# Re-sorting the head of a fused attention and expert kernel: values before keys, and one step of the first tile between the two halves of the second

## The chip, the cores and the metric

The kernel runs on one core of a Trainium2 chip. The metric is the device time of one execution in microseconds (us); lower is better. TensorE is called PE below (PEld is its weight load), VectorE is DVE, ScalarE is ACT, GpSimd is POOL and SyncE is SP.

## What is computed

The reference is banded attention over 8 batches, 8 heads, 576 positions and a head dimension of 64, followed by one feed-forward layer with the ELU function on all 4608 tokens:

```
scores = q @ k^T / 8, kept where |i - j| <= 32, else -1e9
attn   = softmax(scores);  a = attn @ v
x = a.transpose(0, 2, 1, 3).reshape(4608, 512)
h = x @ w_in                      # 512 x 2048
g = where(h > 0, h, exp(min(h, 0)) - 1)
out = g @ w_out                   # 2048 x 512
```

All inputs and the output are float32; the kernel multiplies in bfloat16.

## The kernel before

**Units of work.** Attention goes by *pairs*: pair i is two blocks of 64 queries, all heads, so 128 tokens. There are 36 pairs. The feed-forward layer goes by *tiles* of 256 tokens, two pairs to a tile, 18 tiles. Each tile has 8 *steps*; a step is 256 of the 2048 hidden columns. The list `order` (line 700) gives the order of the steps kk = 0, 1, 2, ...: steps 0 and 1 are the first two of tile 0, steps 2 and 3 the first two of tile 1, steps 4 and 5 the third and fourth of tile 0, steps 6 and 7 those of tile 1, and so on. From tile 2 on the tiles follow one another.

**One pair.** `scores` (line 372) makes the products of queries and keys in PSUM; `exponential` (393) applies the exponential on ACT. For the first four pairs `band` (360) has written a large negative number outside the band ahead of the products; later pairs are multiplied by a mask (`mask`, 400). `pv` (409) multiplies by the values, with a column of ones that gives the denominators; `normalize` (423) divides on DVE (a reciprocal, line 426, and a product, line 429). `x_transpose` (434) turns the 128 tokens' x on PE into PSUM, and `x_evac` (451) copies it to the bfloat16 tile xT, on ACT or DVE as its argument says (`copy_on`, lines 289 to 293).

**One step.** `mm1` (706) makes h in PSUM: 8 matmuls of 256 tokens (line 744), or, for steps 2 and 3, twice 8 matmuls of 128 tokens, one set for each pair of tile 1 (`BY_PAIRS`). `exponents` (750) takes the exponential on ACT (line 754) and calls `subtract` (759), which takes 1 off: on ACT for steps 1, 3 and 4 (line 764), on DVE for the rest (line 766; for step 0 only later, inside `elu`). `elu` (769) joins both branches on DVE and writes the tile g (line 777). `mm2(n)` (823) adds step n's g times w_out to the tile's two sums psY, 128 tokens each, in 4 matmuls of 512 columns (line 797).

**Order.** The schedule is written out by hand (`manual_schedule`): each engine runs its instructions in the order in which the program emits them. `at(kk, slot, fn, ...)` (572) puts a function into a slot of step kk: "half" is after the first 4 of the 8 matmuls of `mm1`, "mid" after `mm1` with its exponents, "dve" before it, "end" at the end. The loop at line 850 emits, for each step: `elu` of a listed step, slot "dve", `mm1`, slot "mid", `mm2` of listed steps, slot "end". Two small dictionaries (lines 852 and 864) change the lists in the first steps.

**The head.** Lines 484 to 545 are emitted ahead of the loop. Queries and keys of batch 0 come in three parts: HALF_A first through SP's and ACT's queues, FRONT_B through POOL's queue as a load that converts (`load_cast`, line 138, tile c), FRONT_C later. `transpose_qk` (328) turns a part on PE and copies it to qT or kT; `front_transpose` (472) does so in two halves, each with an engine and a PSUM tag of its own. Pairs 0 and 1 need HALF_A alone; pairs 2 and 3 need FRONT_B. Values come as V_e and V_o, two layouts that differ by 64 rows; in the first batch POOL loads V_o (`load_v_odd`, 157) and DVE copies parts of it to V_e (`rotate_back`, 163).

**POOL's queue.** Lines 488 to 501 and 547 to 559 issue the loads that convert: parts of q and k, values, and the weights. `load_w_in(c, z, nz)` (197) loads part z of nz of the c-th quarter (512 columns) of w_in; `load_w_out` likewise. After the last part of w_in a small load on SP's queue (`gate`, line 192) holds back SP's loads of the next batches' q and k (tile f).

**PSUM.** Tiles are named by tag: "s" and "u" have two banks, "y0", "y1", "h0", "h1" one. The tag "u" is given up at step 5 (`swap_pools`, line 84), and its two banks become "h2" and "t0", the sums of tile 1; tile 0's sums are "y0" and "y1". A tile of a tag waits until the readers of the tag's former tile are done.

Of the kernel before, what the change touches and what calls it, by code (L numbers as in the profile page):

```python
# [21 lines left out]
def kernel(  # L22
# [9 lines left out]
    nc = tc.nc  # L32
# [86 lines left out]
    FRONT_B = ((NC * HJ, HJ - 2), (NC * HJ, HJ - 1))  # L119
# [37 lines left out]
    def load_v_odd(b, m):  # L157
        lo = 128 * m + WIN
        nc.gpsimd.dma_start(  # L159
            out=V_o[b % 3][:, m, :, 0:D],  # L160
            in_=v[b, :, lo:lo + 128, :].rearrange("h p d -> p h d"))

    def rotate_back(b, m0, m1, parts=(0, 1)):
        e, o = V_e[b % 3], V_o[b % 3]
        for z in parts:
            nc.vector.tensor_copy(e[64 * (1 - z):64 * (2 - z),
                                    m0 + z:m1 + z],
                                  o[64 * z:64 * (z + 1), m0:m1])
# [28 lines left out]
    def load_w_in(c, z=0, nz=1):  # L197
        w = D_FF // 4 // nz
        c = c * nz + z
        nc.gpsimd.dma_start(  # L200
            out=w_in_sb[:, :, c * w:(c + 1) * w],
            in_=moe_w_in[:, c * w:(c + 1) * w].rearrange(
                "(o p) f -> p o f", p=128))
# [124 lines left out]
    def transpose_qk(b, which, part, j0, n, evac, tag="t0", later=None,  # L328
                     pt=None):
        z, nj = part  # L330
        if pt is None:
            pt = ps_tile([128, 1024 if n <= 8 else 2048], BF16, tag, "ptx")
        for j in range(n):
            if (b, which, z) in qk_c:
                for h in range(2):
                    nc.tensor.transpose(
                        pt[64 * h:64 * (h + 1), j * 128:(j + 1) * 128],
                        qk_c[b, which, z][:, h, (j0 + j) * D:
                                          (j0 + j + 1) * D], ident)
            else:  # L340
                nc.tensor.transpose(  # L341
                    pt[:, j * 128:(j + 1) * 128],
                    qk_b[b, which, z][:, j0 + j, :], ident)

        def evict(d=None, rows=NC, pitch=S):
            d = keys_or_queries(b, which) if d is None else d
            copy_on(evac,
                    _bap(d, [d.ap[0], [pitch, HP], [nj, rows], [1, n]],
                         z + j0),
                    _bap(pt, [pt.ap[0], [1, HP], [HP, rows], [128, n]]))  # L350

        if later is None:
            evict()
        else:
            later.append(evict)
# [4 lines left out]
    def band(i, tag):  # L360
        psS = ps_tile([128, 2, 512], FP32, tag, "psS")
        banded[i] = psS, tag
        step = QB if i == 0 else 0
        for par in range(2):
            nc.tensor.matmul(
                _bap(psS, [psS.ap[0], [128, HP], [QB, 2], [1, QB]], par * 512),
                lhsT=ident,
                rhs=_bap(far, [far.ap[0], [0, HP], [step, 2], [1, QB]],
                         QB - step),
                start=True, stop=False)  # L370
# [38 lines left out]
    def pv(i):  # L409
        psS, pu, pm, _, _ = st[i]  # L410
        for h in range(H):
            hp, par = h // 2, h % 2
            for z in range(2):
                jb = 2 * i + z
                b, qb = jb // NQB, jb % NQB
                vv = (V_e if qb % 2 == 0 else V_o)[b % 3]
                nc.tensor.matmul(  # L417
                    psS[QB * z:QB * (z + 1), par, hp * VD:(hp + 1) * VD],
                    lhsT=pm[:, par * HP + hp, z * QB:(z + 1) * QB],
                    rhs=vv[:, qb // 2, h, :],  # L420
                    start=True, stop=True)
# [12 lines left out]
    def x_transpose(i, bank=None):  # L434
        x_st, tag = st[i][3:]
        tag = bank or tag
        pt = ps_tile([128, NDO, 128], BF16, tag, "psXT")
        for do in range(NDO):
            nc.tensor.transpose(
                pt[:, do, :], x_st[:, 2 * do:2 * do + 2, :], ident)  # L440
        st[i] = pt
# [9 lines left out]
    def x_evac(i, eng=nc.vector):  # L451
        copy_on(eng, xT_of(i), st.pop(i))
# [19 lines left out]
    def front_transpose(which, part, evacs, tags, later=None):  # L472
        for (j0, n), evac, tag in zip(split(part), evacs, tags):
            transpose_qk(0, which, part, j0, n, evac, tag, later)
# [13 lines left out]
    for which in range(2):  # L488
        load_cast(0, which, FRONT_B[which])
    load_w_in(0, 0, 2)  # L490
    for m in (2, 3):
        load_v_odd(0, m)
    for z in (2, 3):
        load_w_in(0, z, 4)
    load_w_in(1)
    load_w_out(0, 0, 2)
    load_w_out(0, 1, 2)
    load_v(0, 4, HIGH)
# [6 lines left out]
    BOTH = (nc.scalar, nc.vector)  # L505
# [16 lines left out]
    for m in range(2):  # L522
        for z in range(2):
            rotate_back(0, m, m + 1, (z,))
    pv(0)
    front_transpose(0, FRONT_B[0], (nc.scalar, nc.scalar), ("h0", "h1"),
                    later := [])
    pv(1)
    later.pop(0)()
    for i in (0, 1):  # L530
        normalize(i)
    later.pop(0)()
    front_transpose(1, FRONT_B[1], BOTH, ("y0", "y1"))
    for i in (0, 1):
        x_transpose(i, f"h{i}")
        x_evac(i, BOTH[i])
        if i == 0:
            band(2, "s")
    scores(2)
    exponential(2)  # L540
    band(3, "u")
    scores(3)
    exponential(3)
    rotate_back(0, 2, 3)
    rotate_back(0, 3, 4, (0,))

    load_w_in(2, 0, 2)
    load_w_out(1, 1, 2)
# [23 lines left out]
    def at(kk, slot, fn, *args):  # L572
        tasks.setdefault((kk, slot), []).append((fn, args))

    def run(kk, slot):
        for fn, args in tasks.get((kk, slot), ()):
            fn(*args)
# [7 lines left out]
        at(kk + 2, "end", x_evac, i, nc.scalar)  # L585


    for i in (2, 3):
        at(0, ("half", "mid")[i - 2], pv, i)
        at(0, ("half", "mid")[i - 2], normalize, i)  # L590
    at(1, "half", x_transpose, 2, "y0")
    at(1, "half", x_evac, 2, nc.scalar)
    at(1, "mid", x_transpose, 3, "y1")
    at(1, "mid", x_evac, 3, nc.vector)
    at(5, "dve", swap_pools)


# [36 lines left out]
    for i in range(4, NPAIR):  # L634
        two = i >= FIRST_TWO
        kk, z = begin[i], i % 2 if two else 0
# [68 lines left out]

    def mm1(kk):
        t, s = order[kk]
        if kk == BY_PAIRS[1]:
            return
        ks = BY_PAIRS if kk == BY_PAIRS[0] else (kk,)  # L710
        tags = ((f"h{kk % 2}", "s") if kk == NSTEP - 1 else
                ("s",) if kk == 2 else ("u",) if kk == 3 else (f"h{kk % 2}",))
        for k in ks:
            psH[k] = []
        for z, tag in enumerate(tags):
            for k in ks:
                psH[k].append(ps_tile([128, FG // len(tags), TT], FP32,
                                      tag if k == kk else "u", "ps"))
        for p in range(len(ks)):
            for k in ks:  # L720
                for z in range(len(tags)):
                    products(k, z, p if len(ks) > 1 else None)
                if p == len(ks) - 1:
                    for z in range(len(tags)):
                        exponents(k, z)
                        if k == NSTEP - 1:
                            elu(k, z)


    BY_PAIRS = (2, 3)  # L730

    def products(kk, z, pair):
        t, s = order[kk]
        ps = psH[kk][z]
        w = ps.shape[1]
        for j in range(w):
            fo = s * FG + z * w + j
            for do in range(NDO):
                if pair is None:
                    o, r = ps[:, j, :], xT[t][:, :, do, :]  # L740
                else:
                    o = ps[:, j, pair * 128:(pair + 1) * 128]
                    r = xT[t][:, pair, do, :]
                nc.tensor.matmul(  # L744
                    o, lhsT=w_in_sb[:, do, fo * 128:(fo + 1) * 128],
                    rhs=r, start=(do == 0), stop=(do == NDO - 1))
            if j == 0 and pair is None:
                run(kk, "half")
# [100 lines left out]

    for kk in range(NSTEP):  # L850
        run(kk, "first")
        for n in {1: (), 2: (0, 1), 9: ()}.get(kk, (kk - 1,)):
            if n >= 0:
                elu(n)
        run(kk, "dve")
        mm1(kk)
        run(kk, "mid")
        if kk == NSTEP - 1:
            last_sums()
        elif kk >= LATE + LAG:  # L860
            for _ in range(3 if kk < LATE + LAG + 4 else 4):
                add(*todo.pop(0))
        else:
            for n in {2: (), 3: (), 4: (), 5: (0, 2), 6: (1, 3), 7: (4,),
                      8: (5, 6)}.get(kk, (kk - LAG,) if kk >= LAG else ()):
                run(kk, n)
                mm2(n)
        run(kk, "end")
# [30 lines left out]
```

## Time and profile before

| | us |
|---|---|
| median of 3 runs | 302.36 (302.04 to 302.88) |
| the profiled execution | 303.15 |
| its span, first to last instruction | 301.4 |
| PE busy in the span | 291.4 |
| DVE, ACT, POOL busy | 241.2, 169.0, 56.8 |
| start of step 0's matmuls (L744) | 15.38 |
| start of steps 2 and 3's matmuls | 19.00 |
| start of the first sums (L797) | 22.54 |

The granted TensorE clock was 0.998 of full speed in the mean. In a row of the timeline the columns are: start, duration, engine, line, operation, output<-inputs, sizes, how many, and in brackets the engine's idle time before it with what ended that. In a row of the waits they are: who waited for what, us in total, how many times, the longest. Matmul ends are modelled and overlap with the next start.

### The profile page before, as it was taken

The page shows a single profiled execution, that of the slowest core. Times are in us where ns is not written, and L with a number is a line of the kernel's source. Part 1 is how long each engine was busy: PE and PEld are TensorE (multiplying, and loading weights), DVE is VectorE, ACT ScalarE, POOL GpSimd, SP SyncE. Part 2 cuts the span into 40 slices and gives each one's busy share as a digit, 9 for nine tenths or more (in the row PEclk, how much of TensorE's full clock was granted, in tenths as well). Part 3 has the DMA queues.
Part 4 walks back from the last instruction along what each step waited for, and adds up shares of the span by engine and source line. Part 5 has one row for each costly group of instructions (what it writes and reads, how often), then busy time and mean ns, then how long its engine had stood idle before and what let it go on. Part 6 is the DMA issues. An engine that isn't in the chain of part 4 may idle for free.

```text
span 301.4 us, 7665 instructions
## 1 busy us (share of the span) xinstructions
PE 291.4 (97%) x3064; PEld 198.7 (66%) x3116; DVE 241.2 (80%) x478; ACT 169.0 (56%) x256; POOL 56.8 (19%) x81
## 2 busy tenths in 40 slices
PE   8899999999999999999999999999999999999995
PEld 3586666676666666666666666666666666666673
DVE  7776787988788988988888879887988787876773
ACT  3773458688655567456754675467535353534342
POOL 8778613620005000320022002300000000000000
PEclk9999999999999999999999999999999999999999
DMA  9999999999967978999899979996921121111011
GB/s 190 168 199 178 190 226 410 367 155 217 231 177 169 268 118 242 228 290 145 161 265 316 178 186 256 323 153 127 279 51 72 35 72 38 70 37 70 2 70 71
DMA packets 94645, 52.74 MB, mean 175 GB/s; under 512 B 78226, under 2 KB 84370, under 8 KB 94610
## 3 DMA queue, kind: packets, MB, share of 16 engines
q0 software_dynamic: 45552, 10.03, 45.2%
q1 hardware_dynamic: 47330, 35.74, 44.9%
q10 hardware_dynamic: 1728, 6.49, 6.1%
q8 instruction: 24, 0.39, 0.6%
q14 instruction: 11, 0.09, 0.1%
HBM read 36.70 MB, written 15.34 MB: 173 GB/s over the span
## 4 chain that ended last, share of the span: by engine, by line
PE 74%; DMA 13%; issue 3%; POOL 3%; DVE 2%; ACT 2%; SPq 0%; POOLq 0%; ACTq 0%; DVEq 0%
PE ps L744 34%; PE psY L797 34%; DMA w_out_sb<-in_moe_w_out_dram 4%; PE psS L417 3%; DMA w_in_sb<-in_moe_w_in_dram 3%; DMA out_dram<-y_sb 3%; PE psS L385 2%; DMA c<-in_k_dram 2%; DMA f<-in_q_dram 2%; ACT e_sb L754 1%; DVE g_sb L777 1%; POOL Ve L152 1%; POOL Vo L159 1%; DVE m_sb L766 0%; POOL w_out_sb L208 0%
## 5 line engine op out<-in xcount | busy, mean ns | idle before, releaser
L744 PE MATMUL ps<-xT,w_in_sb 128*128 128x256 bf16 (+1 forms) x1168 | 149.5, 271 | 0.2 <-DMA w_in_sb<-in_moe_w_in_dram 0.2
L754 ACT ACTIVATE e_sb<-ps 128x512 f32<-128x512 f32 (+1 forms) x145 | 86.1, 595 | 113.2 <-PE ps L744 104.4
L797 PE MATMUL psY<-w_out_sb,g_sb 128*128 128x512 bf16 (+2 forms) x541 | 138.9, 373 | 2.8 <-issue 0.3
L744 PEld LDWEIGHTS <-w_in_sb 128*128 128x128 bf16 x1168 | 110.5, 98 | 36.7 <-DMA w_in_sb<-in_moe_w_in_dram 0.3
L777 DVE SCALAR_TENSOR_TENSOR g_sb<-ps,m_sb 128x512 bf16<-128x512 f32 (+1 forms) x145 | 99.3, 686 | 13.3 <-DVE m_sb L766 0.5
L766 DVE TENSOR_SCALAR m_sb<-e_sb 128x512 bf16<-128x512 f32 (+1 forms) x142 | 61.0, 430 | 33.5 <-ACT e_sb L754 31.3
L797 PEld LDWEIGHTS <-g_sb 128*128 128x128 bf16 x592 | 56.1, 98 | 38.8
L152 POOL DMA_DIRECT2D Ve<-in_v_dram x37 | 32.4, 888 | 128.4 <-PE psS L417 79.5
L396 ACT ACTIVATE pu<-psS 128x1024 bf16<-128x1024 f32 x36 | 36.5, 1020 | 1.4 <-PE psS L385 1.4
L429 DVE TENSOR_TENSOR x_st<-psS,rc 128x512 bf16<-128x512 f32 x36 | 24.9, 691 | 1.2
L291 ACT CAST qkb<-f 128x768 bf16<-128x768 f32 (+2 forms) x29 | 25.1, 864 | 0.8 <-DMA f<-in_q_dram 0.8
L405 DVE TENSOR_TENSOR pm<-pu,masks 128x1024 bf16<-128x1024 bf16 x32 | 21.8, 681 | 0.5 <-ACT pu L396 0.5
L417 PEld LDWEIGHTS <-pm 128*64 128x64 bf16 x512 | 9.6, 110 | 7.3 <-DVE pm L405 6.9
L293 DVE COPY y_sb<-psY 128x512 f32<-128x512 f32 (+1 forms) x18 | 12.2, 676 | 1.5 <-PE psY L797 1.5
L385 PEld LDWEIGHTS <-kT 64*128 64x128 bf16 x560 | 9.4, 95 | 4.8 <-issue 4.0
L385 PE MATMUL psS<-qT,kT 64*128 64x64 bf16 x560 | 11.9, 191 | 0.4 <-DVE y_sb L293 0.2
L291 ACT COPY y_sb<-psY 128x512 f32<-128x512 f32 (+1 forms) x19 | 10.8, 566 | 2.5 <-PE psY L797 2.5
L417 PE MATMUL psS<-Ve,pm 128*64 128x65 bf16 x288 | 11.5, 196 | 0.1
L417 PE MATMUL psS<-Vo,pm 128*64 128x65 bf16 x224 | 10.3, 196 | 0.0
L176 DVE COPY Vo<-Ve 64x1040 bf16<-64x1040 bf16 (+2 forms) x22 | 9.1, 414 | 0.7
L291 ACT COPY qT<-ptx 128x512 bf16<-128x512 bf16 (+4 forms) x7 | 6.3, 938 | 3.9 <-PE ptx L341 3.1
L426 DVE RECIPROCAL rc<-psS 128x8 f32<-128x8 f32 x36 | 7.1, 198 | 0.7 <-PE psS L417 0.7
(58 smaller groups left out, 96.1 us busy)
## 6 DMA issues: line engine op xcount, KB each, us to landing
out_dram<-y_sb SPq DMA_DIRECT2D x36, 256.0 KB, 4.0
f<-in_q_dram SPq DMA_DIRECT2D x12, 576.0 KB, 6.6
f<-in_k_dram SPq DMA_DIRECT2D x12, 576.0 KB, 8.3
in_dram<-qkb ACTq DMA_DIRECT2D x10, 576.0 KB, 4.2
Ve<-in_v_dram POOLq DMA_DIRECT2D x21, 128.0 KB, 12.5
w_out_sb<-in_moe_w_out_dram POOLq DMA_DIRECT2D x8, 256.0 KB, 8.4
Ve<-in_v_dram POOLq DMA_DIRECT2D x14, 96.0 KB, 11.1
w_in_sb<-in_moe_w_in_dram POOLq DMA_DIRECT2D x5, 256.0 KB, 7.5
```

The source lines that it names most:

```text
L152: nc.gpsimd.dma_start(out=V_e[b % 3][p0:p1, m, :, 0:D], in_=v[b, :, lo + p0:lo + p1, :].rearrange("h p d -> p h d"))
L291: nc.scalar.copy(d_, s_)
L385: nc.tensor.matmul(psS[:, h % 2, hp * 128 + z * QB:hp * 128 + (z + 1) * QB], lhsT=keys, rhs=qT[b % 2][base:base + 64, hp, QB * qb:QB * (qb ...
L396: nc.scalar.activation(pu, _bap(psS, [psS.ap[0], [1, 1024]]), AX.Exp, scale=SCALE)
L405: nc.vector.tensor_mul(pm, pu, _bap(mm, [mm.ap[0], [0, H], [1, 2 * QB]]))
L417: nc.tensor.matmul(psS[QB * z:QB * (z + 1), par, hp * VD:(hp + 1) * VD], lhsT=pm[:, par * HP + hp, z * QB:(z + 1) * QB], rhs=vv[:, qb // 2 ...
L429: nc.vector.tensor_mul(x_st, _bap(psS, [psS.ap[0], [VD, HP], [512, 2], [1, D]]), _bap(rc, [rc.ap[0], [2, HP], [1, 2], [0, D]]))
L744: nc.tensor.matmul(o, lhsT=w_in_sb[:, do, fo * 128:(fo + 1) * 128], rhs=r, start=(do == 0), stop=(do == NDO - 1))
L754: nc.scalar.activation(e_sb, ps, AX.Exp)
L766: nc.vector.tensor_scalar(m_sb, e_sb, -1.0, None, ALU.add)
L777: nc.vector.scalar_tensor_tensor(g_t[kk][:, z * w:(z + 1) * w, :], ps, 0.0, m_t.pop((kk, z)), ALU.max, ALU.min)
L797: nc.tensor.matmul(sum_of(t, ts, c), lhsT=g_t[n][:, j, ts * 128:(ts + 1) * 128], rhs=w_out_sb[:, s * FG + j, cols_of(c)], start=(s == 0 an ...
```

## The change

The change moves work in the head and in the first steps; it adds one load (a weight load split in two) and no arithmetic.

1. POOL's queue: the values' load `load_v_odd(0, 3)` goes behind two loads of w_in, and `load_w_in(1)` becomes two halves.
2. The head: `pv(1)` directly after `pv(0)`; FRONT_B's queries in one piece with one copy on ACT; then pair 0's x and pair 2's band, and only then FRONT_B's keys. Pair 0's x copy moves from ACT to DVE, pair 1's from DVE to ACT. One `rotate_back` leaves the head.
3. Pair 2's x moves from the middle of `mm1(1)` to behind it (slot "mid"), with its copy on ACT as before; pair 3's values move from step 0 to the same slot, behind the `rotate_back` that they need; pair 3's x moves to a new slot "pair", after both steps' products for tile 1's first pair, and its copy goes from DVE to ACT.
4. `mm1(4)`, tile 0's third step, is emitted between the two halves of steps 2 and 3, in the PSUM tag "y1" instead of "h0".
5. The order of `elu` becomes 0, 1, 4, 2, 3, 5 (before: 0, 1, 2, 3, 4, 5), and `mm2` of steps 2, 1, 3, 4 comes a little later: step 5 adds step 0, step 6 adds 2 and 1, step 7 adds 3 and 4.

```
     load_w_in(0, 0, 2)
-    for m in (2, 3):
-        load_v_odd(0, m)
+    load_v_odd(0, 2)
     for z in (2, 3):
         load_w_in(0, z, 4)
-    load_w_in(1)
+    load_v_odd(0, 3)
+    load_w_in(1, 0, 2)
+    load_w_in(1, 1, 2)
...
-    pv(0)
-    front_transpose(0, FRONT_B[0], (nc.scalar, nc.scalar), ("h0", "h1"),
-                    later := [])
-    pv(1)
-    later.pop(0)()
+    for i in (0, 1):
+        pv(i)
+    transpose_qk(0, 0, FRONT_B[0], 0, FRONT_B[0][1], nc.scalar, "h0")
     for i in (0, 1):
         normalize(i)
-    later.pop(0)()
+    x_transpose(0, "h1")
+    x_evac(0, nc.vector)
+    band(2, "s")
     front_transpose(1, FRONT_B[1], BOTH, ("y0", "y1"))
-    for i in (0, 1):
-        x_transpose(i, f"h{i}")
-        x_evac(i, BOTH[i])
-        if i == 0:
-            band(2, "s")
+    x_transpose(1, "h0")
+    x_evac(1, nc.scalar)
...
     rotate_back(0, 2, 3)
-    rotate_back(0, 3, 4, (0,))
...
-    for i in (2, 3):
-        at(0, ("half", "mid")[i - 2], pv, i)
-        at(0, ("half", "mid")[i - 2], normalize, i)
-    at(1, "half", x_transpose, 2, "y0")
-    at(1, "half", x_evac, 2, nc.scalar)
-    at(1, "mid", x_transpose, 3, "y1")
-    at(1, "mid", x_evac, 3, nc.vector)
+    at(0, "half", pv, 2)
+    at(0, "half", normalize, 2)
+    at(1, "mid", x_transpose, 2, "y0")
+    at(1, "mid", x_evac, 2, nc.scalar)
+    at(1, "mid", rotate_back, 0, 3, 4, (0,))
+    at(1, "mid", pv, 3)
+    at(1, "mid", normalize, 3)
+    at(3, "pair", x_transpose, 3, "y0")
+    at(3, "pair", x_evac, 3, nc.scalar)
...
-                ("s",) if kk == 2 else ("u",) if kk == 3 else (f"h{kk % 2}",))
+                ("s",) if kk == 2 else ("u",) if kk == 3 else
+                ("y1",) if kk == BETWEEN else (f"h{kk % 2}",))
...
         for p in range(len(ks)):
+            if p == 1:
+                mm1(BETWEEN)
             for k in ks:
                 for z in range(len(tags)):
                     products(k, z, p if len(ks) > 1 else None)
+                if p == 0:
+                    run(k, "pair")
...
-        for n in {1: (), 2: (0, 1), 9: ()}.get(kk, (kk - 1,)):
+        for n in {1: (), 2: (0, 1), 3: (4,), 4: (2, 3), 5: (),
+                  9: ()}.get(kk, (kk - 1,)):
...
-            for n in {2: (), 3: (), 4: (), 5: (0, 2), 6: (1, 3), 7: (4,),
+            for n in {2: (), 3: (), 4: (), 5: (0,), 6: (2, 1), 7: (3, 4),
                       8: (5, 6)}.get(kk, (kk - LAG,) if kk >= LAG else ()):
```

`BETWEEN` is 4. `mm1(3)` and `mm1(4)` emit nothing when the loop comes to them, since their products have been made.

More of the change, by code (lines that the diff above doesn't have):

```diff
@@ L707, in mm1 @@
         t, s = order[kk]
-        if kk == BY_PAIRS[1]:
+        if kk in psH:
             return
@@ L727, in mm1 @@
                             elu(k, z)
-    BY_PAIRS = (2, 3)
+    BY_PAIRS, BETWEEN = (2, 3), 4
     def products(kk, z, pair):
```

## The prediction

> **What bounds the kernel now.** I read the busy times of the page first, then the waits of PE, then each engine's timeline over the first 26 us, and the waits around the one late gap. Times are us from the span's start; "issue" of a row is from its start to the next row's start, because a matmul's last 0.16 us or so lie under the next one.
>
> ```profile
> PE 291.4 (97%) x3064; PEld 198.7 (66%) x3116; DVE 241.2 (80%) x478; ACT 169.0 (56%) x256; POOL 56.8 (19%) x81
> ```
> PE is busy for 97% of the span. So what counts is where PE stands still:
> ```profile
> PE ptx L336 <- DMA c<-in_q_dram: 0.8, 1, 0.8
> PE ptx L336 <- DMA c<-in_k_dram: 0.4, 1, 0.4
> PE ptx L341 <- ACT xT L291: 0.4, 1, 0.4
> PE ps L744 <- DMA w_in_sb<-in_moe_w_in_dram: 0.2, 1, 0.2
> ```
> Three of these lie in the front that the change re-sorts (before 11.34, 12.61 and 17.50), one at 47.80. After 19.00 there is no other real gap: any delay of PE's stream there reaches the end. The rest is a question of order on each engine. PE (first rows of its weight loads, then rows of its matmuls):
> ```profile
> 11.34 0.42 PEld L336 LDWEIGHTS <-c 128*64 128x64 bf16 x14 [0.88 <-DMA c<-in_q_dram]
> 12.61 0.48 PEld L336 LDWEIGHTS <-c 128*64 128x64 bf16 x16 [0.54 <-DMA c<-in_k_dram]
> 14.16 0.29 PEld L385 LDWEIGHTS <-kT 64*128 64x128 bf16 x16
> ```
> ```profile
> 18.17 0.60 PE L744 MATMUL ps<-xT,w_in_sb 128*128 128x256 bf16 x4
> 18.61 0.39 PE L439 MATMUL psXT<-ident,x_st 128*128 128x128 bf16 x4
> 19.00 3.69 PE L744 MATMUL ps<-xT,w_in_sb 128*128 128x128 bf16 x48
> 22.54 1.89 PE L797 MATMUL psY<-w_out_sb,g_sb 128*128 128x512 bf16 x7
> ```
> The 48 are steps 2 and 3 by pairs (32 of 128 columns) and steps 4 and 5 (16 of 256), without a pause. ACT, in its own order:
> ```profile
> 18.37 0.59 ACT L291 COPY xT<-psXT 128x512 bf16<-128x512 bf16 x1 [0.82 <-PE psXT L439]
> 18.85 0.60 ACT L754 ACTIVATE e_sb<-ps 128x512 f32<-128x512 f32 x1
> 19.49 0.63 ACT L764 ACTIVATE m_sb<-e_sb 128x512 bf16<-128x512 f32 x1
> ```
> To be seen: pair 2's x copy runs **ahead** of step 1's exponential and subtraction, and ends at 18.95, just before PE takes it at 19.00.
> ```profile
> 46.00 1.26 ACT L291 CAST qkb<-f 128x1280 bf16<-128x1280 f32 x1 [0.83 <-DMA f<-in_q_dram]
> 47.17 0.58 ACT L291 COPY xT<-psXT 128x512 bf16<-128x512 bf16 x1
> ```
> This is what PE waits for at 47.80: a transfer, not PE's own work.
>
> **What the Trainium skill says.** "TensorE: Matmul & The Clock Gate", Back-to-back issue gap, gives N/2.4 + 2.5 ns for a warm matmul of N columns alone, 109 ns for 256 and 56 for 128, but warns of about 81 at 128 with weight loads between. The trace sides with the first: 8 matmuls of 256 take 0.88 us of issue (24.26 to 25.14), and the block of 48 (19.00 to 22.54, 3.54 us) less 16 x 0.109 leaves 0.056 for each of the 32 narrow ones. "Perfetto Trace Analysis", Optimization Strategy, says to find the gaps on the busiest engine and what blocks each; that is what I do. "DMA: Bandwidth & Descriptors", Anatomy of one DMA, says that DMA engines just consume their queues and that waits happen at the issuer; here the landings do come in the order of issue, 0.3 to 2.4 us apart, so a load put earlier in POOL's queue should land earlier. "PSUM — Partial Sum Buffer", The four PSUM rules, says that GpSimd cannot read PSUM; so x copies are left to ACT or DVE, as all L291/L293 rows show.
>
> **The change part by part.**
>
> *Front order.* No instruction is added; pair 1's values, pair 0's x transposes and pair 2's band go ahead of the keys' transposes. Pair 1's exponential ends at 10.94 (9.00 + 1.94); 0.10 later, as for pair 0, pv(1) starts at 11.04, takes 0.38 (15.92 to 16.30 in pair 2's rows): 11.42. The 14 query transposes take 0.36 (11.34 to 11.70): 11.78. Pair 0's x is normalized at 11.76 (11.07 + 0.69), so its 4 transposes run 11.85 to 12.07; the band takes 0.44 (13.41 to 13.85): 12.51. The keys land at 12.57 (issue 5.72, 6.8 to landing), so their transposes start at 12.61 **as before**. The gaps of 0.77 and 0.43 are filled, but what is late next is the keys themselves: transposes, then DVE's copy 13.29 to 13.98 (DVE is free by 13.12, after pair 1's normalize and pair 0's x copy), then scores(2). These started at 14.16 behind x transposes that now run before the copy is done, so at about 14.06. Gain 0.1; bounds 0 and 0.2. mm1(0) then starts at 15.28 instead of 15.38. The one ACT copy of 7 x 128 in place of two ends near 12.95, as the two did.
>
> *POOL's queue.* One odd load moves behind two quarter loads of w_in, and w_in(1) becomes two halves: one issue more, 0.77 us of POOL (an L200 row) under transfers that take longer; cost on the path 0. The two quarters landed at 17.45 and 17.79 (8.91 + 8.5, 9.66 + 8.1); the load ahead of them took about 1.06 of the queue, so they land near 16.4 and 16.7, before their use at 16.74 and 17.2: the 0.20 gap goes. If they do not move: +0.7. The odd load lands near 17.8; DVE's copy of it (0.29) feeds pv(3). SP's queue is not touched.
>
> *First tile.* mm1(0) with pv(2) inside takes 0.54 + 0.38 + 0.54 (rows 15.38, 15.92, 16.30): done at 16.74. mm1(1) follows at once, 0.87: 17.61. Pair 2's transposes 0.22: 17.83. pv(3) waits for DVE's copy (18.11): 18.17 to 18.55. Then PE wants pair 2's x. But x_evac(2) is now emitted after step 1's exponents, on the same engine. ACT: exponential from 17.84 to 18.44, the m_sb activation to 19.10 (0.63 plus 0.03), the copy about 19.02 to 19.60. First products of pair 2 at 19.65: PE stands 1.1 us, a **new wait**, and is 0.65 behind 19.00. Behind it in PE's queue is everything.
>
> *Step 4 between the pairs.* Both pairs' first half: 16 x 0.056 = 0.90 (20.55). Pair 3's x transposes, formerly before 19.00: 0.22 (20.77). mm1(4) 0.87 (21.64). ACT's copy of pair 3's x (0.59 from 20.98) is hidden under it. Second half 0.90 (22.54), mm1(5) 0.87 (23.41). Before, this point was 22.54: +0.87.
>
> *y1.* Step 4's psum is now "y1", which is also the second sum of tile 0. mm2(0) runs its first half on y0 (2 x 0.217 = 0.43, to 23.84); its second half needs elu(4) to have read y1. ACT after mm1(4): e_sb(4) 21.84 to 22.44, m_sb(4) to 23.10, e_sb(2) to 23.60. DVE's order is fixed: m_sb(2) comes before elu(4), so 23.63 to 24.06, then 0.69 to 24.78. PE goes on at 24.84: a second **new wait** of 1.0, with mm1(6) and all after it behind. If the wait is put ahead of the whole of mm2(0): 1.43. If it vanished: 0. Taken: 1.0. The new order of the sums costs nothing: the same seven mm2 are done when transpose_casts starts. u's two banks (h2, t0) come free with elu(3) near 26.06, PE wants them at 26.14. mm2(6) ends at 33.07 against 31.20: +1.87.
>
> *47.80.* The loads f hang on the last w_in, not on PE; they land at 45.93 as before, while PE comes at 49.26. The 0.41 is absorbed.
>
> Sum: -0.10 (front) + 0.75 (first wait, net of the removed 0.20 and of pv(3) filling in) + 0.22 + 1.0 - 0.41 = **+1.46**. The profiled execution took 303.15 with a span of 301.4; the span would be 302.9 and that execution 304.6. It is 0.8 above the median of the runs, 302.36; I add the sum to the median: **303.8**.
>
> **The rivals.** A measurement of this kernel tells about 0.3%, 0.9 us, from no change.
> *Only the first wait comes.* If elu(4) is done when PE gets to y1 (DVE finishing a microsecond sooner), the sum is +0.46: 302.8, no change. For it: PE has other work between, 2.2 us from mm1(4)'s end. Against: the chain of ACT and DVE rows above is 3.2 us long from there, all durations measured. Chance 0.13, with larger front gains counted in.
> *PE fills up and nothing new waits (faster).* ACT is idle 44% of the span, so the copy of pair 2's x may slip in early; the removed gaps (0.77 + 0.43 + 0.20, and 0.17 at 19.00) would put PE 1.57 ahead: 300.8. It decides at two readings of one stream: the copy done by 18.55, and, since PE would then come to 47.39 early and wait for f, f landing before about 45.0. Against: ACT's rows run in program order, and f's landing does not depend on PE. Chance 0.07.
> *The weights stay late.* The quarters land at 17.45 anyway, or y1 holds up all of mm2(0): 0.7 or 0.43 more, 304.3 to 304.9. Chance 0.2, part of slower.
> *The forecast:* 0.6, with its own range 303.2 to 304.3 (front 0 to 0.2, and the 0.41 kept or not).
>
> **How the numbers follow.** Slower 0.6 + 0.2 = 0.80, same 0.13, faster 0.07. The range reaches down into the first rival, 302.5, and up to the third, 305.0; outside lie the faster case and a little on either side.
>
> **What would show it.** Right: PE's keys' transposes still at 12.6; ACT's order e_sb, m_sb, xT near 18 to 19.6, and a PE wait of about 1.1 on ACT's xT; a PE wait of about 1.0 on DVE's g_sb near 24.8 at L797; no wait at 47 to 50. Wrong: PE's pair-2 products before 19.2; psY's second sum running on without a pause; f landing much earlier, or a w_in wait near 17.

## The result, and the profile after

The changed kernel takes 303.88 us (303.81 to 304.2, 6 runs) against 302.39 (301.73 to 302.88, 6 runs): a ratio of 1.0054, with a 95% interval of 1.004 to 1.0067. It is slower by 1.49 us. The profiled execution took 304.2 with a span of 302.5.

Line numbers after the change: L750 is the former L744 (step matmuls), L760 the exponential, L770 and L772 the subtraction on ACT and on DVE, L783 the joining on DVE, L803 the sums.

Who PE waited for, in the changed kernel (four of six rows; us in total, times, longest):

```profile
PE ps L750 <- ACT xT L291: 1.2, 1, 1.2
PE psY L803 <- DVE g_sb L783: 1.0, 1, 1.0
PE psS L385 <- DVE kT L293: 0.6, 1, 0.6
PE psS L417 <- ACT pu L396: 0.4, 1, 0.4
```

The prediction's four waits (for the loads c, for the weights, and the one at 47.80) are gone. Two waits of a microsecond on other engines have come, and two shorter ones in the head. PE's matmuls around them:

```profile
17.51 0.39 PE L439 MATMUL psXT<-ident,x_st 128*128 128x128 bf16 x4
...
19.50 1.05 PE L750 MATMUL ps<-xT,w_in_sb 128*128 128x128 bf16 x16 [1.22 <-ACT xT L291]
20.39 0.39 PE L439 MATMUL psXT<-ident,x_st 128*128 128x128 bf16 x4
20.61 2.80 PE L750 MATMUL ps<-xT,w_in_sb 128*128 128x256 bf16 x32
23.25 0.59 PE L803 MATMUL psY<-w_out_sb,g_sb 128*128 128x512 bf16 x2
24.84 0.59 PE L803 MATMUL psY<-w_out_sb,g_sb 128*128 128x512 bf16 x2 [0.99 <-DVE g_sb L783]
```

The first wait is ACT's order. Its timeline:

```profile
17.71 0.60 ACT L760 ACTIVATE e_sb<-ps 128x512 f32<-128x512 f32 x1 [0.28 <-PE ps L750]
18.34 0.63 ACT L770 ACTIVATE m_sb<-e_sb 128x512 bf16<-128x512 f32 x1
18.88 0.57 ACT L291 COPY xT<-psXT 128x512 bf16<-128x512 bf16 x1
...
46.34 0.60 ACT L760 ACTIVATE e_sb<-ps 128x512 f32<-128x512 f32 x1 [1.63 <-PE ps L750]
46.84 1.25 ACT L291 CAST qkb<-f 128x1280 bf16<-128x1280 f32 x1
```

Pair 2's transposes are done at 17.90, but the copy starts only at 18.88, behind the exponential and the subtraction. The conversion at 46.84 answers to the one at 46.00 before: it no longer waits for the loads f, since they landed (45.35) before ACT came to it. The second wait is DVE's order:

```profile
23.46 0.73 DVE L772 TENSOR_SCALAR m_sb<-e_sb 128x512 bf16<-128x512 f32 x1 [2.46 <-ACT e_sb L760]
24.11 1.87 DVE L783 SCALAR_TENSOR_TENSOR g_sb<-ps,m_sb 128x512 bf16<-128x512 f32 x3
```

DVE was idle for 2.46 us while step 4's inputs became ready (ACT's m_sb of step 4 ends at 22.94); it stood at step 2's subtraction, and only then joined step 4 (the first of the three in the second row), which freed y1 for PE at 24.84.

Where the time went can be read from three marks of PE: step 0's first matmul, the transposes of the parts c near 31 to 33 (L336 for the second time), and the query transposes of batch 1 (L341, near 48). The last stretch differs little between these two.

| kernel profiled | keys landed | step 0 | step 0 to L336 | L336 to L341 | L341 to the end | span |
|---|---|---|---|---|---|---|
| before | 12.57 | 15.38 | 15.91 | 16.51 | 253.6 | 301.4 |
| changed | 12.16 | 15.27 | 17.89 | 15.84 | 253.5 | 302.5 |

The second stretch has grown by 1.98, the third has shrunk by 0.67. These two executions differ by 1.05 (303.15 and 304.2), less than the medians' 1.49: the one before was slow for its kernel, by 0.8, the one after by 0.3.

### The profile page after: what moved, and what is told of

Read it like the earlier page. It is cut to its first block, busy times and chain, and to the rows that moved or that the text cites. A ratio compares the mean times of both kernels' runs of the same rounds, so it can differ in the third digit from the quotient of the medians.

```text
span 302.5 us, 7715 instructions
## 1 busy us (share of the span) xinstructions
PE 293.8 (97%) x3116; PEld 198.2 (66%) x3116; DVE 240.3 (79%) x477; ACT 169.4 (56%) x256; POOL 57.7 (19%) x82
## 4 chain that ended last, share of the span: by engine, by line
PE 93%; ACT 2%; DVE 2%; DMA 1%; issue 0%; DVEq 0%; ACTq 0%
PE ps L750 41%; PE psY L803 41%; PE psS L417 4%; PE psS L385 4%; DMA f<-in_q_dram 1%; PE ptx L341 1%; ACT pu L396 1%; PE ptx L336 1%; DVE qkb L293 1%; PE psXT L439 1%; PE psS L365 1%; ACT e_sb L760 1%; DVE m_sb L772 0%; DVE pm L405 0%; DVE kT L293 0%
## 5 line engine op out<-in xcount | busy, mean ns | idle before, releaser
L750 PE MATMUL ps<-xT,w_in_sb 128*128 128x256 bf16 (+1 forms) x1168 | 149.4, 271 | 1.2 <-ACT xT L291 1.2
L760 ACT ACTIVATE e_sb<-ps 128x512 f32<-128x512 f32 (+1 forms) x145 | 86.2, 595 | 113.3 <-PE ps L750 106.5
L803 PE MATMUL psY<-w_out_sb,g_sb 128*128 128x512 bf16 (+2 forms) x592 | 147.4, 374 | 1.0 <-DVE g_sb L783 1.0
L750 PEld LDWEIGHTS <-w_in_sb 128*128 128x128 bf16 x1168 | 110.7, 98 | 37.4 <-issue 1.2
L783 DVE SCALAR_TENSOR_TENSOR g_sb<-ps,m_sb 128x512 bf16<-128x512 f32 (+1 forms) x145 | 99.1, 685 | 12.7 <-DVE m_sb L772 0.5
L772 DVE TENSOR_SCALAR m_sb<-e_sb 128x512 bf16<-128x512 f32 (+1 forms) x142 | 61.5, 433 | 35.7 <-ACT e_sb L760 33.8
L803 PEld LDWEIGHTS <-g_sb 128*128 128x128 bf16 x592 | 56.1, 98 | 39.9 <-issue 1.3
L291 ACT COPY qT<-ptx 128x1152 bf16<-128x1152 bf16 (+4 forms) x6 | 6.1, 1033 | 4.0 <-PE ptx L341 3.1
```

The lines of the kernel that those rows point to most:

```text
L291: nc.scalar.copy(d_, s_)
L750: nc.tensor.matmul(o, lhsT=w_in_sb[:, do, fo * 128:(fo + 1) * 128], rhs=r, start=(do == 0), stop=(do == NDO - 1))
L760: nc.scalar.activation(e_sb, ps, AX.Exp)
L772: nc.vector.tensor_scalar(m_sb, e_sb, -1.0, None, ALU.add)
L783: nc.vector.scalar_tensor_tensor(g_t[kk][:, z * w:(z + 1) * w, :], ps, 0.0, m_t.pop((kk, z)), ALU.max, ALU.min)
L803: nc.tensor.matmul(sum_of(t, ts, c), lhsT=g_t[n][:, j, ts * 128:(ts + 1) * 128], rhs=w_out_sb[:, s * FG + j, cols_of(c)], start=(s == 0 an ...
```

## The experiments

The theory: two new waits, each from the order on another engine, cost PE about 2 us; a part of it is absorbed at 47.8, where the kernel before waits for the loads f. The rivals are told with the runs. Three sets of four kernels ran, each set on one chip with its own runs of the kernel before (medians 302.21, 302.07 and 302.13); ratios are against those. The result came from runs of its own, so against the changed kernel's 303.88 the ratios are the better guide.

**1. The first wait.** In the changed kernel, step 1's subtraction goes behind pair 2's copy.

```
-        if kk > 0:
+        if kk > 1:
             subtract(kk, z)
...
-        if kk == 0:
+        if kk <= 1:
             subtract(kk, z)
```

> The changed kernel, with step 1's subtraction of 1 (ACT, 0.63 us) emitted behind pair 2's x copy instead of ahead of it; nothing else. Theory (the copy is late because of ACT's order): the copy ends at 18.80 instead of 19.45, pair 2's products start at 18.85 instead of 19.50; then pair 3's products have to wait for pair 3's normalize (19.35) to leave the bank u, so 0.55 of the 0.65 stays. Time 303.9 - 0.55 = 303.3. Rival (the wait is for something else, pv(3) or the x transposes): 303.9, and products still at 19.5.

Measured: 303.74 (303.42 to 303.91), ratio 1.0052 (1.004 to 1.0064). The trace does what the theory said:

```profile
17.71 0.60 ACT L760 ACTIVATE e_sb<-ps 128x512 f32<-128x512 f32 x1 [0.28 <-PE ps L750]
18.20 0.58 ACT L291 COPY xT<-psXT 128x512 bf16<-128x512 bf16 x1
18.67 0.64 ACT L770 ACTIVATE m_sb<-e_sb 128x512 bf16<-128x512 f32 x1
```

The products start at 18.83 instead of 19.50. The two first halves then take 1.19 instead of 1.05, which fits the expected wait for u, and pair 3's transposes follow at 19.86 instead of 20.39: 0.53 of the 0.67 is left there, as expected. The second wait is 0.88 instead of 0.99, and L341 comes at 48.35 instead of 49.00. The order on ACT is the cause of the first wait. The time expected, 303.3, was not reached: the ratio is that of the changed kernel (1.0054) within its interval, so a gain in time is not shown by this run.

**2. The second wait.** Step 4's elu directly behind `mm1(4)`; then, in a second kernel, mm2(1) ahead of mm2(2) as well.

```
                 mm1(BETWEEN)
+                elu(BETWEEN)
...
-        for n in {1: (), 2: (0, 1), 3: (4,), 4: (2, 3), 5: (),
+        for n in {1: (), 2: (0, 1), 3: (), 4: (2, 3), 5: (),
```

and in the second kernel also

```
-            for n in {2: (), 3: (), 4: (), 5: (0,), 6: (2, 1), 7: (3, 4),
+            for n in {2: (), 3: (), 4: (), 5: (0,), 6: (1, 2), 7: (3, 4),
```

> The changed kernel, with step 4's elu emitted on DVE directly behind mm1(4), so ahead of step 2's subtraction; nothing else. Theory (y1 is held by elu(4), and elu(4) by its place on DVE): elu(4) ends at 23.66 instead of 24.8, the second half of mm2(0) runs on without a pause; next in the way is mm2(2), whose bank comes free with elu(3) at about 25.5, where PE would be at 25.0. PE gains 24.84 - 23.68 = 1.0 there and gives 0.4 back: 303.9 - 0.6 = 303.3. Rival (elu(4) is late because ACT is, not because of DVE's order): the pause stays, 303.9.

> As the run with step 4's elu first, and mm2(1) ahead of mm2(2) in step 6, so that mm2(2)'s bank is not wanted before elu(3) is done. Theory: the 0.4 that mm2(2) takes back comes too: 303.9 - 1.0 = 302.9. Rival (no such wait on the bank): the same as without the swap.

Measured: 303.57 (303.44 to 303.79) and 303.21 (303.09 to 303.72), ratios 1.0049 (1.0037 to 1.0061) and 1.0039 (1.0027 to 1.0051). With the elu first, PE's rows are:

```profile
23.25 1.06 PE L804 MATMUL psY<-w_out_sb,g_sb 128*128 128x512 bf16 x4
24.15 1.04 PE L751 MATMUL ps<-xT,w_in_sb 128*128 128x256 bf16 x8
25.57 1.67 PE L804 MATMUL psY<-w_out_sb,g_sb 128*128 128x512 bf16 x7 [0.38 <-DVE g_sb L784]
```

The pause inside mm2(0) is gone (x4 without a break), and 0.38 stands in front of mm2(2) in its place: that stall moved to the next thing that was late, the bank that elu(3) frees. With the sums swapped:

```profile
24.15 1.04 PE L751 MATMUL ps<-xT,w_in_sb 128*128 128x256 bf16 x8
25.02 1.89 PE L804 MATMUL psY<-w_out_sb,g_sb 128*128 128x512 bf16 x8
```

no wait is left there. L341 comes at 48.42 and 47.89, against 49.00: 0.58 and 1.11, where 0.6 and 1.0 were expected. (The expectation's 24.84 - 23.68 is 1.16, not 1.0.) The times are both 0.3 above those expected. DVE's order is the cause of the second wait, and ACT (the rival) is not.

**3. Both.** The edits of 1 and of the second kernel of 2 together.

> Both together: step 1's subtraction behind the x copy, step 4's elu first, mm2(1) ahead of mm2(2). Theory: the two waits are the whole loss; -0.55 and -1.0 add up to 302.35, the time of the kernel before, and PE's arrival at the query transposes of batch 1 is again ahead of the loads f, so that a wait of 0.2 to 0.5 stands there again. Rival (the re-sorted head has made PE faster and only the two waits hid it): below 301.9.

Measured: 302.66 (302.42 to 303.94), ratio 1.0018 (1.0008 to 1.0029): 0.45 above the kernel before. L341 comes at 47.47, 1.53 ahead of the changed kernel; expected were 1.55. So the two waits are most of the loss, but perhaps not all: the interval runs from 0.2 to 0.9. The gains in time don't add up run by run: against 1.0054 the ratio fell by 0.0002 without the first wait, by 0.0015 without the second, and by 0.0036 without both. PE's marks do add up (0.65, 1.11, 1.53, the last with a wait of 0.56 on pair 2's copy left), and the ratios have intervals of 0.001 either way. The expectation that PE would again meet a wait for f failed: the loads had landed at 45.21, and no wait of that kind is in the trace. The next runs look for the rest, 0.45, in the head.

**4. The head.** The changed kernel with the old head (the head's hunk of the change, from `pv` to pair 1's x copy, taken back); and the old kernel with that hunk alone:

```
-    pv(0)
-    front_transpose(0, FRONT_B[0], (nc.scalar, nc.scalar), ("h0", "h1"),
-                    later := [])
-    pv(1)
-    later.pop(0)()
+    for i in (0, 1):
+        pv(i)
+    transpose_qk(0, 0, FRONT_B[0], 0, FRONT_B[0][1], nc.scalar, "h0")
...
```

> The changed kernel with the head of the kernel before (queries' transposes ahead of pv(1), keys' transposes ahead of pair 0's x and pair 2's band); POOL's queue and the steps as changed. Theory (the head's order is worth 0.1 at most, since the keys gate): 303.9 + 0.1 = 304.0, step 0 at about 15.4. Rival (what now stands ahead of the keys' transposes delays them when the keys land early, as in the profile after, 12.16 against 12.53): 303.9 - 0.3 = 303.6, step 0 at about 15.0. Rival (the filled gaps count in full): 303.9 + 0.7 or more.

> The kernel before with the changed head alone (with the odd values' copy kept where it was); POOL's queue and the steps as before. Theory: 302.4, no change, because step 1 waits for its weights at 17.45 in any case, and PE waits for the loads f at 47.8 in any case. Rival (the filled gaps count): 301.7 or less.

Measured: the old head in the changed kernel 303.97, but from 303.05 to 304.88; ratio 1.0053 (1.0035 to 1.0072). This settled nothing, since the changed kernel did not run on that chip. Its trace was a hint: step 0 at 14.81. The new head in the old kernel: 302.12 (301.82 to 304.12), ratio 1.0005 (0.9989 to 1.002), no change, as expected, but not for the reasons given. Neither of the two waits that the expectation rests on is in its trace: the weights had landed at 15.98 and 16.69, the loads f at 44.58, and PE went on to L341 (line numbers shift by 3) without a pause:

```profile
46.23 1.03 PE L794 MATMUL psY<-w_out_sb,g_sb 128*128 128x512 bf16 x4
47.09 0.72 PE L341 MATMUL ptx<-ident,qkb 128*128 128x128 bf16 x10
```

The old head was then run again beside the changed kernel.

> The changed kernel as it is, on the chip on which the next three run. Theory: 303.9, step 0 at 15.27 whatever the hour at which the keys land, since pv(1), pair 0's x and the band stand ahead of their transposes. Rival (its head follows the landing as the old one does): step 0 and the time scatter as those of the kernel before.

> The changed kernel with the old head, beside the changed kernel on one chip. Theory now (from the first run of it: keys landed at 11.99, step 0 at 14.81 against 15.27, and PE came to the query transposes 0.76 earlier): with both new waits in place nothing takes a gain back before 47, so where the keys land near 12.0 it is 0.4 to 0.8 faster than the changed kernel, 303.1 to 303.5, with more scatter. Rival (the head is worth 0.1, as forecast): 303.8 to 304.0.

Measured on one chip: changed 304.07 (303.74 to 304.69), with the old head 303.17 (303.06 to 304.1); ratios 1.0065 (1.0048 to 1.0081) and 1.0043 (1.0027 to 1.0058). The re-sorted head **costs** the changed kernel 0.9 by these medians, and 0.7 by the ratios, whose intervals overlap. PE comes to L341 at 49.00 with the new head (49.64 in a second profile, where the keys landed late) and at 48.24 and 48.06 with the old one. The first run with the old head (1.0053) did not show the gain in time. Why the head costs, is seen in the weight loads of PE. Changed kernel (the first profile after):

```profile
11.00 0.34 PEld L417 LDWEIGHTS <-pu 128*64 128x64 bf16 x16 [0.54 <-ACT pu L396]
11.25 0.43 PEld L336 LDWEIGHTS <-c 128*64 128x64 bf16 x14
11.77 0.23 PEld L439 LDWEIGHTS <-x_st 128*128 128x128 bf16 x4
11.95 0.15 PEld L365 LDWEIGHTS <-ident 128*128 128x128 bf16 x2
12.53 0.47 PEld L336 LDWEIGHTS <-c 128*64 128x64 bf16 x16 [0.42 <-DMA c<-in_k_dram]
```

Old head in the changed kernel:

```profile
10.12 0.34 PEld L417 LDWEIGHTS <-pu 128*64 128x64 bf16 x16 [0.42 <-ACT pu L396]
10.38 0.42 PEld L336 LDWEIGHTS <-c 128*64 128x64 bf16 x14
10.99 0.34 PEld L417 LDWEIGHTS <-pu 128*64 128x64 bf16 x16 [0.19 <-ACT pu L396]
11.75 0.48 PEld L336 LDWEIGHTS <-c 128*64 128x64 bf16 x16 [0.43 <-DMA c<-in_k_dram]
```

In the second run the keys had landed at 11.71 and PE took them at 11.75, after a real wait. (In the changed kernel the 0.42 in the last row is only the load path's pause while PE runs the band; the keys had landed before, and PE has no gap there.) In the new head they are not taken before 12.53, whether they land at 12.16 (here) or at 11.27 (the kernel of experiment 3): pv(1), which waits for ACT's exponential to 10.95, the queries, pair 0's x and the band stand ahead. It is a floor, and no more than that: in the repeated profile of the changed kernel the keys landed at 13.43, and step 0 was at 16.21, so the expectation that it stands at 15.27 "whatever the hour" was wrong on the late side.

**5. Both waits away, and the old head.** The edits of 3, with the head's hunk taken back.

> The changed kernel with both waits taken away and the old head. Theory (the 0.45 that the version without waits still lost is the new head's floor): 302.2, as the kernel before. Rival (it is the one wait on pair 2's copy that is left, 0.56, and the head has no part): 302.6.

Measured: 302.44 (301.89 to 303.3), ratio 1.0005 (0.9987 to 1.0022): by the ratio level with the kernel before, though the median is 0.3 above it, between the theory's 302.2 and the rival's 302.6. So the new head is a likely part of what was left in experiment 3, and this run does not show that it is all: the interval reaches 0.7, and overlaps that of experiment 3. Its profile caught an execution with late loads (f at 46.18), and there the old wait is back. ACT:

```profile
46.26 1.26 ACT L291 CAST qkb<-f 128x1280 bf16<-128x1280 f32 x1 [0.83 <-DMA f<-in_q_dram]
47.42 0.58 ACT L291 COPY xT<-psXT 128x512 bf16<-128x512 bf16 x1
```

PE stood for 0.41 behind that copy, as before the change at 47.80.

**6. The wait for f.** The kernel before with pair 5's x copy on DVE, so that it isn't behind the conversion; and the same in the kernel without the two waits.

```
-            at(*x_at, x_evac, i, nc.scalar)
+            at(*x_at, x_evac, i, nc.vector if i == 5 else nc.scalar)
```

> The kernel before with pair 5's x copy on DVE instead of ACT, so that it does not stand behind the conversion that waits for the loads f; nothing else. Theory (PE's wait at 47.80 is a transfer that also swallows what PE gains earlier): the query transposes start at 47.32 instead of 47.80, 302.4 - 0.4 = 302.0. Rival (the wait costs nothing or DVE's later work takes it back): 302.4.

> The changed kernel with both waits taken away (subtraction behind the copy, elu(4) first, mm2(1) ahead of mm2(2)) and pair 5's x copy on DVE. Theory: PE comes to the query transposes about 0.3 later than in the kernel before, at 47.5, and goes on at once: 302.1, a little above the kernel before with that copy alone. Rival (the changed order of the head and of step 4 is worth something once nothing hides it): 301.7 or less.

Measured: 302.52 (301.61 to 303.64), ratio 1.0015 (1.0005 to 1.0025), and 304.3 (303.75 to 306.52), ratio 1.0076 (1.005 to 1.0102). Both expectations failed. DVE's own order was overlooked: a rotation of values (0.56 us) stands ahead of the copy there, and PE waited 0.47 for DVE instead of for ACT. Why the first kernel is slower than before, if only a little, is open. In the second the same 0.47 is in the profile, but that execution had its first keys late, at 7.3, a stretch at half clock (see the end), and step 0 at 17.91. The mean clock of its other five runs was 0.997 or more, so why they are all over 303.7 is open. Then the rotation went behind the copy:

```
-        at(14 + z, "dve", rotate_v, 1, 1, VS - 1, (z,))
+        at(14 + z, ("dve", "mid")[z], rotate_v, 1, 1, VS - 1, (z,))
...
-            at(*x_at, x_evac, i, nc.scalar)
+            at(*x_at, x_evac, i, nc.vector if i == 5 else nc.scalar)
```

> The kernel before with pair 5's x copy on DVE, and the second half of a rotation of values that stood ahead of it on DVE (0.56 us) moved behind it; the earlier try had that rotation ahead, so that DVE's copy ended no earlier than ACT's. Theory (PE's wait ahead of the query transposes takes back what is gained earlier): PE goes on at the end of ACT's conversion, some 0.5 earlier, 301.6. Rival (the rotation is missed later, or PE arrives there no earlier): 302.1 or more.

Measured: 301.95 (301.13 to 302.43), ratio 0.9987 (0.9974 to 1.0001): 0.2 less by the medians, 0.4 by the ratio, and the interval just reaches no change. PE's rows:

```profile
45.55 1.03 PE L797 MATMUL psY<-w_out_sb,g_sb 128*128 128x512 bf16 x4
46.41 0.72 PE L341 MATMUL ptx<-ident,qkb 128*128 128x128 bf16 x10
...
52.73 0.41 PE L385 MATMUL psS<-qT,kT 64*128 64x64 bf16 x16 [0.36 <-DVE y_sb L293]
```

The wait is gone (46.41 follows at once), and 0.36 is given back later, at the DVE copy that frees pair 7's bank; the profile before had 0.2 there. It is the fastest version of all these, but not shown to be faster than the kernel before.

PE's marks in all of them, with its three stretches (us):

| kernel profiled | keys landed | step 0 | to L336 | to L341 | to the end |
|---|---|---|---|---|---|
| changed, subtraction behind copy | 12.03 | 15.27 | 17.25 | 15.83 | 253.4 |
| changed, elu of step 4 first | 11.98 | 15.27 | 17.31 | 15.84 | 253.4 |
| the same, sums swapped | 11.77 | 15.27 | 16.78 | 15.84 | 253.5 |
| changed, second profile | 13.43 | 16.21 | 17.59 | 15.84 | 253.3 |
| changed, both waits away | 11.27 | 15.27 | 16.25 | 15.95 | 253.4 |
| changed, old head (two profiles) | 11.99, 11.71 | 14.81, 14.53 | 17.59, 17.70 | 15.83 | 253.4 |
| both waits away, old head | 12.25 | 15.07 | 16.32 | 16.66 | 253.6 |
| before, new head | 12.21 | 15.51 | 15.74 | 15.83 | 253.5 |
| before, pair 5 on DVE | 11.79 | 14.61 | 15.64 | 16.60 | 253.3 |
| the same, rotation behind | 11.35 | 14.92 | 15.64 | 15.85 | 253.8 |
| both waits away, pair 5 on DVE | 11.54 | 17.91 | 16.33 | 16.47 | 254.1 |

## Why the prediction was right, and where it was not

The forecast, +1.46, came from two new waits, and the runs show both, with their causes.

- **The first wait.** Forecast: 1.1 us, products at 19.65. Measured: 1.22 and 19.50. The order on ACT is shown to be the cause (experiment 1). The odd values landed at 17.28 and not near 17.8, so pv(3) was not held up; the wait took that time over.
- **Step 4 between the pairs.** PE's stream from 19.50 to mm1(5)'s end at 23.25 takes 3.75, forecast 3.76 (19.65 to 23.41). Pair 3's copy lay under mm1(4), as forecast.
- **The second wait.** Forecast: 1.0, PE on at 24.84. Measured: 0.99, 24.84, only ahead of the second half of mm2(0). DVE's order is shown to be the cause (experiment 2). That the sizes agree to a hundredth is luck: the row counts from the modelled end of the matmul ahead, the forecast from when PE could issue, and so counted the wait is 1.16 (from 23.68). PE was 0.16 early, and DVE's subtraction, started 0.17 early, took 0.65 to the next row and not 0.43. The wait for u's banks, forecast as just missed, appeared as soon as the pause was taken away.
- **The stretch from step 0 to L336** was forecast to grow by 1.97 (1.87 at its end, and 0.10 at its start); it grew by 1.98.
- **What is absorbed** was mis-sized: forecast 0.41, measured 0.67 between the two profiles. I took the idle time from the row, but that counts from the modelled end of the matmul ahead, and PE issues 0.16 before that end when nothing holds it: the wait was worth 0.57. The other 0.1 is pair 4's x, for which PE waited at 38.86 in the profile before, so there was a small gap after 19.00 that the prediction did not see.
- **The head** is the step that failed. The forecast was a gain of 0.1, bounds 0 and 0.2. Step 0 came at 15.27, forecast 15.28, but through another gate: the keys were forecast to hold their transposes until 12.61, and in fact they had landed at 12.16, and what held them to 12.53 was the band ahead. So the hundredth is luck. And the profile before was of an execution in which the keys landed late, at 12.57. The five other profiles with the old head, of the kernel before or the changed one with edits, have them at 11.35 to 12.25, and step 0 at 14.53 to 15.07; the new head does not use that. Its cost in the changed kernel, 0.7 to 0.9 on one chip, was not in the sum. I read one landing time as if it were a constant of the program, though the profiled execution's 303.15 stood 0.8 above the median, and the prediction said so. On the third chip 8 of the 28 runs of the kernel before took 303.0 or more, and the other 20 at most 302.53; a time of 303.15 would be among the 8.
- **The weights** moved forward, further than forecast: the quarters landed at 15.01 and 15.79 (forecast 16.4 and 16.7), and no wait for them is left. About 1 us of this is the new place in the queue, as forecast: where the keys landed as late under the old queue (12.21, the new head in the kernel before), the quarters came at 15.98 and 16.69. The rest is the late execution again. In the three other profiles with the old queue no step waits for these weights, so the 0.20 that the sum took off was not a wait of every execution.

The forecast of the total, 303.8 against 303.88, is closer than its parts, and in that there is luck. For the profiled execution the same sum gave 304.6, and 304.2 was measured: 0.26 too little was taken as absorbed. Added to the median the sum came out right; the likely reason, argued and not shown, is that the head costs more in the usual execution than in the late one that was read. On the third set's chip, where the difference was 1.94, it would have been 0.5 off.

Where did the gain of the filled gaps go? No run shows that it was there to have. In the kernel before, the new head starts step 0 at 15.51, later than the old head in the five profiles above, and loses nothing (1.0005). What gives the time back there is argued from profiles of its variants, not shown, since the kernel before itself was profiled once, and late: with the old head an earlier PE is stopped ahead of L341. In the kernel with pair 5's x on DVE, step 0 was at 14.61 and PE stood until 46.84; there ACT's conversion waited for f (landed at 44.92) and ended at 46.26, so a copy behind it on ACT (0.49 more, as before the change) would have ended at about the same time, 46.75 by this estimate. With the new head PE came to the same place at 47.09, so 0.90 at step 0 had become 0.25. That f can hold PE there is seen in the profile before and in experiment 5; that it does so in every execution, as I had assumed, is not so (experiment 4). In the changed kernel PE comes there at 48 to 50, after the loads, with either head, so nothing is given back, and the same head costs 0.7 to 0.9. Taking the wait away gained 0.2 to 0.4 in the kernel before, and the interval has room for anything from none to 0.8.

## What to carry to other kernels

When a step is moved from inside another to behind it, list what the other emits on the engine of the moved step: here one copy went from ahead of 1.2 us of ACT's work to behind it, and one PSUM tag was handed to a tile whose reader stood behind another step's subtraction on DVE. A gap that waits for a transfer should not be filled with work that the engine's order puts in front of the transfer's user: where the data come earlier than in the profiled run, the filling becomes the wait. So compare the profiled execution with the median of the runs before its landing times go into a sum. And before an early gain is counted, look for the next fixed arrival downstream; it absorbs gains and losses alike, until the loss is larger than the slack.

## What the runs showed of the hardware

The landing times of the same loads, at the same place of the same queue, differ from run to run: the keys, issued at 5.7 in each of the 14 profiles, landed between 11.27 and 13.43.

One profiled execution (both waits away, pair 5 on DVE) had a granted TensorE clock of 0.50 from 9.11 to 12.53 us. In every other profile the clock was 1.00 in that stretch. Its band matmuls took about twice the usual time, 1.82 us for the 4 against 1.03, and it was 2.6 us later at step 0 than the kernel without that copy. In the 3.41 us ahead of the slow stretch PE was busy for 1.59 us, against 2.78 in the changed kernel and 3.02 in the kernel without that copy; its longest pause there was only 1.08, for late keys. One execution shows no rule. I had expected neither.
